# Other order of the first block's maxima, and one query tile summed among the first scores

## The chip, the core and the metric

The kernel runs on one core of one Trainium2 chip. The metric is the device time of one execution in microseconds (us), the median of several runs. Five engines work side by side: TensorE (PE, with its weight loads shown apart as PEld), VectorE (DVE), ScalarE (ACT), GpSimd (POOL) and SyncE (SP), which here issues the DMAs. Each engine works through its instructions in order and waits for the others through semaphores.

## The reference

Four attention layers follow one another, each added to its input: A, B, A, B. S = 2048 tokens, D = 576 features, H = 32 heads of Dh = 18.

```python
def _A_ref(x, wqkv, wo):                      # 32 key heads
    qkv = (x @ wqkv).reshape(B, S, 3, H, Dh).transpose(2, 0, 3, 1, 4)
    q, k, v = qkv[0], qkv[1], qkv[2]
    p = softmax(einsum("bhqd,bhkd->bhqk", q, k) * Dh ** -0.5)
    o = einsum("bhqk,bhkd->bhqd", p, v)
    return o.transpose(0, 2, 1, 3).reshape(B, S, D) @ wo
# _B_ref: the same with one key head and one value head for all 32 query heads
x = x + _A_ref(layernorm(x), A_wqkv, A_wo)
x = x + _B_ref(layernorm(x), B_wq, B_wk, B_wv, B_wo)
x = x + _A_ref(layernorm(x), A_wqkv, A_wo)
x = x + _B_ref(layernorm(x), B_wq, B_wk, B_wv, B_wo)
```

## The kernel before, in words

The program is written out by hand in the order in which each engine is to work; tiles come from pools with a fixed number of buffers, and a tile that finds no free buffer waits for the reader that frees one. Layers 0 and 2 are of kind A (`is_a`), layers 1 and 3 of kind B.

**A layer in three stages.** First the layer norm's scaled rows are transposed (`scaled`, `trans`; the rows' buffers have the tag `xh`, two of them) into `xts[T]`, four groups T of 512 tokens, and multiplied by the weights. `project(T, t)` (line 432) makes one tile of 128 features by 512 tokens. Each operand is held as a high and a low part, so a tile takes the 14 matmuls of `TERMS` (line 439). ACT copies the sum out (line 447, the high part), a second copy by ACT (line 453) and a subtraction on POOL (line 454) give the low part where the tile is a `filler`, and `store` (lines 499 to 503) writes both to the DRAM buffer `qk_d`: 512 KB for the high part, written twice, and 256 KB for the low one. `load_k`, `load_q` and `load_part` (line 545) bring heads from there into `big`.

Second, the attention loop goes over 16 pairs of heads (a = 0, 1) and four blocks u of 512 queries: 64 blocks w. A block needs the maximum of every score row first. `max_mm` (line 581) makes 128 queries by 512 keys on TensorE (line 613) and reduces them on DVE (line 620); from the third block on some pairs of key blocks are combined with the help of ACT (lines 605, 610, 617). A block has 32 maxima, 16 for each head; (qc, kb) is its part of the queries and its block of keys. After the 32nd, `max_final` makes the negated maxima (line 752), `max_store` transposes them (line 761) and stores them in four small DMAs to `m_d` (line 763), and `max_rows` loads them as rows of `big` (line 767). Then `exp_mm` computes scores with the maxima already subtracted (line 776), ACT takes the exponential (line 785), and `pv_block` sums the values into the PSUM bank `oacc` (line 806). Maxima run ahead of the exponentials by `LEAD` steps, and the value sums lag behind them by `LAG` = 1152 columns, so in the first slots of `UNIT` no value sum is there yet. A slot such as `em` says what each head does (e: a score and its exponential, m, d, t: a maximum), and the number behind it how many columns of value sums follow.

Third, `out_proj` multiplies by the output weights.

**The fill.** The last projections (`fill`) and the maxima that run ahead are woven: `woven(max_pairs, left, every)` lets a burst of four maxima go out after every so many matmuls of the fill. In a layer A it holds eight half value projections (63 units of one 512 column matmul) and four tiles of the last token group (`rest`, 56 units), with 14 bursts; in a layer B two tiles (28 units) and four bursts, and ten bursts lie in the projections before that. `FREE` is the number of units left behind the last burst.

**PSUM banks.** Score tiles come from two tags: `mtile` with three banks, `etile` with four. In a burst before the loop the fourth maximum takes an e bank, the other three m banks. Fill tiles and the scores of `exp_mm` take e banks.

**Order in a layer B.** `m_first` (line 576) gives the order of the maxima of the first two blocks. The keys of the fourth block are made by the first projection of T = 3 and loaded right behind it; bursts come twice in each of the next two projections. `max_store(0, 0)` goes out after 46 maxima and `max_rows(0, 0)` after 50.

**The tile `side`** has the tag `xx`, one buffer, which it shares with `xts[3]`; it holds some exponentials, the combined maxima and the copied value sums, and is taken after the fill.

Of the kernel before, what the change touches and what calls it, by code (L numbers as in the profile page):

```python
# [8 lines left out]
F32 = mybir.dt.float32  # L9
F32R = mybir.dt.float32r  # L10
AF = mybir.ActivationFunctionType
OP = mybir.AluOpType
# [6 lines left out]
P = 128  # L19
NCH = S // P  # L20
NPAIR = H // 2
# [9 lines left out]
TERMS = [(c, c) for c in range(4)] + [(c, 5 + c) for c in range(4)] + [(4, 4), (4, 9)] + [(5 + c, c) for c in range(4)]  # L31
# [13 lines left out]
STEPS = 8  # L45
LEAD = 14

FREE = 4
NM_AT = 3
ROW_AT = 5  # L50
SUM_AT = 4
# [18 lines left out]
LAG = 1152  # L70
# [57 lines left out]
def tile_kernel(ctx: ExitStack, tc: tile.TileContext, A_x, A_wqkv, A_wo, B_x, B_wq, B_wk, B_wv, B_wo, out):  # L128
    nc = tc.nc
# [4 lines left out]
    pool = ctx.enter_context(tc.tile_pool(name="pool", bufs=2))  # L134
# [26 lines left out]
    oacc = psum.tile([P, 512], F32, name="oacc")  # L161
# [27 lines left out]
    def etile(name):  # L189
        return psum.tile([P, 512], F32, tag="e", bufs=4, name=name)  # L190

    def ptile(name, shape=(P, 512), dt=F32):
        return pool.tile(list(shape), dt, tag="p", bufs=15, name=name)

    def xtile(name, shape=(P, 2, 9, 256), dt=F32R):
        return pool.tile(list(shape), dt, tag="xx", bufs=1, name=name)
# [61 lines left out]
    def wtile(t):  # L258
        return parts[(0, 2, 1)[t // 3]][:, t % 3]
# [36 lines left out]
    def woven(f, left, every):  # L296
        assert not weave["left"]
        weave.update(f=f, left=left, every=every, n=0)
# [55 lines left out]
    xts = {}  # L354
# [65 lines left out]
    for layer in range(4):  # L420
        is_a = layer % 2 == 0
# [72 lines left out]
        def store(ev_f, r0, r1, c0, t0):  # L494

            dst = qk_d[c0:c0 + r1 - r0, :, t0:t0 + 512]
            hi, lo = ev_f[0][r0:r1, None, :].to_broadcast([r1 - r0, 2, 512]), ev_f[1][r0:r1, :]
            if c0 < D:
                nc.sync.dma_start(dst[:, 0:3:2], hi)
                nc.sync.dma_start(dst[:, 1], lo)  # L500
            else:
                nc.sync.dma_start(dst[:, 0:2], hi)
                nc.sync.dma_start(dst[:, 2], lo)
# [65 lines left out]
        mxs, nms, pts, ocs = {}, {}, {}, {}  # L569

        def ops(p):
            return big[:, q_slot(p)], big[:, k_slot(p)]

        diffs, m_next, m_done, m_count = ([], []), [0, 0], [0], {}

        m_first = [] if is_a else ([(0, i // 2, i % 2) for i in range(8)] + [(1, i // 2, i % 2) for i in range(4)] +
                                   [(0, i, 2) for i in range(4)] + [(1, i // 2, i % 2) for i in range(4, 6)] +
                                   [(0, i, 3) for i in range(4)] + [(1, i // 2, i % 2) for i in range(6, 8)] +
                                   [(1, i, 2) for i in range(4)] + [(1, i, 3) for i in range(4)])

        def max_mm(a, tile):

            n = m_next[a]
            w, i = divmod(n, 16)
            shared = w >= FIRST_SHARED
            kind = "m"
            if n < len(m_first):
                w, qc, kb = m_first[n]
            elif shared:
                kind, qc, kb = MAX_OPS[a][i]  # L590
            else:
                qc, kb = PLAIN[i]
            p, u = divmod(w, 4)
            q, k = ops(p)
            if (p, u) not in mxs:
                mxs[p, u] = mxd[w % 2] if shared else pool.tile([P, 32], F32, name="mx")
            mx = mxs[p, u]
            b = 64 * a
            c0 = u * 512 + qc * P
            r0 = 16 * a + 4 * qc + kb  # L600
            m_next[a] += 1
            m_done[0] += 1
            if kind == "d":
                ps = etile("psd")
                nc.tensor.matmul(ps, q[b:b + 3 * DH, c0:c0 + P], kds[p if is_a else 0][b:b + 3 * DH],  # L605
                                 start=True, stop=True)
                r = side[:, n_r[0] % 4]
                n_r[0] += 1
                diffs[a].append(r)
                nc.scalar.activation(r, ps, AF.Relu)  # L610
            else:
                ps = tile("psm")
                nc.tensor.matmul(ps, q[b:b + KM, c0:c0 + P], k[b:b + KM, kb * 512:(kb + 1) * 512],  # L613
                                 start=True, stop=True)
                if kind == "t":
                    r = diffs[a].pop(0)
                    nc.vector.tensor_tensor_reduce(out=r, in0=ps, in1=r, scale=1.0, scalar=-3.0e38, op0=OP.add,  # L617
                                                   op1=OP.max, accum_out=mx[:, r0:r0 + 1])
                else:
                    nc.vector.reduce_max(mx[:, r0:r0 + 1], ps, axis=AX.X)  # L620
            m_count[p, u] = m_count.get((p, u), 0) + 1
            if m_count[p, u] == 32:
                max_final(p, u)

        def max_pair():
            if is_a and m_done[0] % 4 == 0:
                run_todo(m_done[0] // 4)
            for a in range(2):
                max_mm(a, etile if m_done[0] % 4 == 3 else mtile)
            if not is_a and m_done[0] == 46:  # L630
                max_store(0, 0)
            elif not is_a and m_done[0] == 50:
                max_rows(0, 0)


# [56 lines left out]
                for h, ps in enumerate(project_v(c)):  # L692
                    nc.scalar.activation(v_dst(c)[:, h], ps, AF.Copy)

        rest = [1, 2, 3, 5] if is_a else [2, 3]
        for T in range(4):
            if T == 0 and not is_a:
                fixed_rows(k_slot(0), True)
# [39 lines left out]
        fill = []  # L738
# [3 lines left out]
                    fill.append((project_v_part, (c, h)))  # L742
        for t in rest:
            fill.append((project, (3, t, True)))

        if is_a:
            load_k(0, 1536, S)
# [2 lines left out]
        def max_final(p, u):  # L750
            neg = pool.tile([P, 8], F32, name="neg")
            nc.vector.tensor_reduce(neg, mxs.pop((p, u)).rearrange("p (b k) -> p b k", k=4), axis=AX.X, op=OP.max,  # L752
                                    negate=True)
            hl = nms[p, u] = hls[(4 * p + u) % 2]
            copy(nc.gpsimd, hl[:, 0:8], neg)
            nc.gpsimd.tensor_tensor(hl[:, 8:16], neg, hl.bitcast(F32)[:, 0:8], op=OP.subtract)  # L756
# [13 lines left out]
        def exp_mm(p, u, i, tile):  # L770

            a, kc = (i // 2) % 2, i // 4 * 2 + i % 2
            q, k = ops(p)
            e = tile("pse")
            r = 64 * a
            nc.tensor.matmul(e, k[r:r + KE, kc * P:(kc + 1) * P], q[r:r + KE, u * 512:(u + 1) * 512],  # L776
                             start=True, stop=True)

            n_p[0] += 1
            r = n_p[0] // 5 % 3  # L780
            own = n_p[0] % 5 or (p, u) == (NPAIR - 1, 3) or sided.get(r) in pts
            pt = pts[p, u, i] = ptile("pt") if own else side[:, 6 + r]
            if not own:
                sided[r] = p, u, i
            nc.scalar.activation(pt, e, AF.Exp, scale=SCALE)  # L785
# [3 lines left out]
        def pv_cols(cols):  # L789

            while cols:
                n, c0 = divmod(pv_at[0], 512)
                w = min(cols, 512 - c0)
                pv_block(n, c0, c0 + w)
                pv_at[0] += w
                cols -= w
# [83 lines left out]
        def run_todo(st):  # L880
            for n in sorted(n for n in todo if n <= st):
                for f, args in todo.pop(n):
                    f(*args)
# [4 lines left out]
        at(b - 1, out_rows, 1)  # L888
        left = LEAD - m_done[0] // 4
        work = len(TERMS) * sum(288 / 512 if f is project_v_part else 1 for f, _ in fill)  # L890
        woven(max_pairs, left, (work - FREE) / left)
        for f, args in fill:
            f(*args)
        assert not weave["left"]
        side = xtile("side", (P, 9, 512), F32)
        late, n_e, n_r, n_p, sided = LAG, 0, [0], [0], {}
        for w in range(4 * NPAIR):
            p, u = divmod(w, 4)
            more_m = w < 4 * NPAIR - 2
            e_next = [0, 0]  # L900
            for kinds, cols in UNIT if more_m else ENDS if w == 4 * NPAIR - 2 else LAST:
                run_todo(LEAD + STEPS * w + sum(e_next) // 4)
                for a in range(2):
                    if kinds[a] == "e":
                        n = e_next[a]
                        e_next[a] += 1
                        exp_mm(p, u, n // 2 * 4 + 2 * a + n % 2, mtile if m_done[0] == 4 * ns and n_e % 7 % 2 else etile)
                        n_e += 1
                    else:
                        max_mm(a, mtile)  # L910
                skip = min(late, cols)
                late -= skip
                pv_cols(cols - skip)
            assert e_next == [16, 16]
        assert not diffs[0] and not diffs[1]
# [39 lines left out]
```

## Time and profile before

| | |
|---|---|
| median of 3 runs | 5605.41 us (5603.79 to 5609.56) |
| the profiled execution's own time | 5606.94 us |
| its span | 5605.2 us |
| mean granted TensorE clock | 0.999 |
| DVE busy | 4943.0 us, 88% |
| ACT busy | 4936.3 us, 88% |
| POOL busy | 1741.9 us, 31% |
| DMA | 291.59 MB, 52 GB/s over the span |

The profile shows one execution. Rows of its timeline read: start in us, duration in us, engine, line of the kernel, operation, output tile from input tiles, shapes, how many instructions were merged into the row; in brackets the idle time of the engine before them and what ended it. Times count from the start of the span. SPq rows are DMAs being issued; they land later. Windows give the busy time of each engine in a stretch, with the number of instructions. A DMA rate row gives GB/s in 40 equal slices of its window.

### The profile page before, as it was taken

Reading aid. Unit: us, or ns where it says so; the run is one execution under the profiler, and the core shown is the slowest. Engines: PE = TensorE matmul, PEld = TensorE weight load, DVE = VectorE, ACT = ScalarE, POOL = GpSimd, SP = SyncE. Lnnn points to the kernel's source line nnn. Section 1 sums busy time; section 2 is a strip of 40 time slices with the busy share of each in tenths; the row PEclk is TensorE's granted clock in tenths of the full one; section 3 lists DMA queues with packets and bytes.
Section 4 is the critical chain, followed back from the end, with each engine's and each line's share of the span. In section 5 each row is a group of like instructions: output and inputs, shape, how many; then the busy total and the mean of one; then the engine's idle time right before and its main releaser. Section 6 shows DMA issues by size and latency. Waiting matters only on the chain.

```text
span 5605.2 us, 138270 instructions
## 1 busy us (share of the span) xinstructions
PE 5579.4 (100%) x53372; PEld 2835.7 (51%) x53372; DVE 4943.0 (88%) x9513; ACT 4936.3 (88%) x9884; POOL 1741.9 (31%) x2236
## 2 busy tenths in 40 slices
PE   9999999999999999999999999999999999999999
PEld 7644444444844444444686444444448444444446
DVE  5799999998699999999747999999987999999995
ACT  3599999999389999999726999999992999999996
POOL 3142323234233232333421332323242333333332
PEclk9999999999999999999999999999999999999999
DMA  6311111111421000001253111111114201010102
GB/s 226 120 47 38 37 39 36 39 36 27 128 68 24 23 21 23 20 23 25 61 188 104 50 36 38 37 39 36 37 31 136 56 23 24 23 24 20 24 14 80
DMA packets 258556, 291.59 MB, mean 52 GB/s; under 512 B 132700, under 2 KB 172892, under 8 KB 248176
## 3 DMA queue, kind: packets, MB, share of 16 engines
q1 hardware_dynamic: 257896, 282.75, 18.0%
q8 instruction: 419, 6.86, 0.5%
q14 instruction: 241, 1.97, 0.1%
HBM read 158.77 MB, written 119.86 MB: 50 GB/s over the span
## 4 chain that ended last, share of the span: by engine, by line
PE 97%; ACT 1%; DVE 1%; DMA 0%; issue 0%; SPq 0%; POOL 0%; ACTq 0%; DVEq 0%; POOLq 0%
PE oacc L806 38%; PE pse L776 23%; PE psm L613 21%; PE psn L280 6%; PE psq L439 6%; PE psd L605 3%; ACT pt L785 1%; PE ps L272 0%; DVE mx L620 0%; DMA big<-m_d 0%; DMA m_d<-tr 0%; PE oacc L273 0%; SPq L763 0%; DVE mxd L620 0%; ACT side L785 0%
## 5 line engine op out<-in xcount | busy, mean ns | idle before, releaser
L620 DVE TENSOR_REDUCE mxd<-psm 128x1 f32<-128x512 f32 x5952 | 3750.1, 683 | 181.5 <-PE psd L605 64.9
L785 ACT ACTIVATE pt<-pse 128x512 f32<-128x512 f32 x6584 | 3578.4, 628 | 28.3 <-PE pse L776 1.5
L613 PE MATMUL psm<-big 62*128 62x512 f32 x7200 | 2504.4, 444 | 0.6
L776 PE MATMUL pse<-big 64*128 64x512 f32 x8192 | 2409.1, 431 | 7.2 <-DMA big<-m_d 3.1
L806 PE MATMUL oacc<-pt,vbuf 128*19 128x192 f32 (+6 forms) x20244 | 1794.5, 379 | 1.2 <-DVE oc L202 1.0
L776 PEld LDWEIGHTS pse<-big 64*128 64x128 f32 x8192 | 1209.2, 184 | 893.8 <-ACT pt L785 517.6
L613 PEld LDWEIGHTS psm<-big 62*128 62x128 f32 x7200 | 1132.7, 184 | 676.7 <-DVE mxd L620 262.2
L806 PE MATMUL oacc<-side,vbuf 128*19 128x64 f32 (+6 forms) x5004 | 1402.5, 377 | 0.0
L785 ACT ACTIVATE side<-pse 128x512 f32<-128x512 f32 x1608 | 998.4, 621 | 5.9
L202 POOL TENSOR_SCALAR hl<-neg 128x8 fp32r<-128x8 f32 x256 | 50.5, 197 | 2746.7 <-DVE neg L752 2746.7
L806 PEld LDWEIGHTS oacc<-pt,vbuf 128*19 128x19 f32 x20244 | 447.8, 97 | 604.8 <-issue 488.7
L617 DVE CUSTOM_DVE_ANT_0 side<-psm,side 128x512 f32<-128x512 f32 x992 | 681.1, 687 | 37.0 <-PE psm L613 8.6
L610 ACT ACTIVATE side<-psd 128x512 f32<-128x512 f32 x992 | 601.3, 648 | 1.3 <-PE psd L605 1.3
L806 PE MATMUL oacc<-pt,vy 128*19 128x384 f32 (+2 forms) x5700 | 587.2, 417 | 0.0
L829 POOL TENSOR_TENSOR rl<-lt,mone 128x8 f32<-128x8 f32 x256 | 422.9, 1652 | 350.2 <-DMA lt<-os 350.2
L806 PE MATMUL oacc<-side,vy 128*19 128x384 f32 (+2 forms) x1404 | 455.7, 415 | 0.0
L605 PE MATMUL psd<-kd,big 54*128 54x512 f32 x992 | 428.0, 472 | 0.0
L806 PEld LDWEIGHTS oacc<-side,vbuf 128*19 128x19 f32 x5004 | 317.4, 97 | 146.4 <-issue 119.8
L447 ACT ACTIVATE ev<-psq 128x512 fp32r<-128x512 f32 (+1 forms) x112 | 66.9, 598 | 319.1 <-PE psq L439 266.6
L842 POOL TENSOR_TENSOR os<-os,rb 96x512 f32<-96x512 f32 x256 | 328.2, 1282 | 19.8 <-DMA rb<-r_d 19.8
L820 POOL TENSOR_TENSOR os<-os,side 96x512 f32<-96x512 f32 x240 | 307.2, 1280 | 20.0
L202 POOL TENSOR_SCALAR os<-side 32x512 f32<-32x512 f32 x480 | 293.7, 612 | 40.1 <-POOL hl L756 0.4
(93 smaller groups left out, 3310.3 us busy)
## 6 DMA issues: line engine op xcount, KB each, us to landing
big<-qk_d SPq DMA_DIRECT2D x180, 432.0 KB
qk_d<-ev SPq DMA_DIRECT2D x96, 512.0 KB
qk_d<-ev SPq DMA_DIRECT2D x120, 256.0 KB
rb<-r_d SPq DMA_DIRECT2D x512, 36.0 KB
o_d<-os SPq DMA_DIRECT2D x512, 36.0 KB
m_d<-tr SPq DMA_DIRECT2D x1024, 2.0 KB
o<-o_d SPq DMA_DIRECT2D x64, 256.0 KB
big<-m_d SPq DMA_DIRECT2D x512, 4.0 KB
```

The costliest lines, as they stand in the source:

```text
L202: eng.tensor_scalar(dst, src, 1.0, 0.0, op0=OP.mult, op1=OP.add)
L280: nc.tensor.matmul(ps, lhs[:, xc, :], wsm[:, wc, h * 288:(h + 1) * 288], start=i == 0, stop=i == len(TERMS) - 1)
L439: nc.tensor.matmul(ps[:n].rearrange("p (u t) -> p u t", u=2)[:, us], w[:, wc, :n], xts[T][:, us, xc, :], start=(xc, wc) == TERMS[0], stop= ...
L605: nc.tensor.matmul(ps, q[b:b + 3 * DH, c0:c0 + P], kds[p if is_a else 0][b:b + 3 * DH], start=True, stop=True)
L610: nc.scalar.activation(r, ps, AF.Relu)
L613: nc.tensor.matmul(ps, q[b:b + KM, c0:c0 + P], k[b:b + KM, kb * 512:(kb + 1) * 512], start=True, stop=True)
L617: nc.vector.tensor_tensor_reduce(out=r, in0=ps, in1=r, scale=1.0, scalar=-3.0e38, op0=OP.add, op1=OP.max, accum_out=mx[:, r0:r0 + 1])
L620: nc.vector.reduce_max(mx[:, r0:r0 + 1], ps, axis=AX.X)
L776: nc.tensor.matmul(e, k[r:r + KE, kc * P:(kc + 1) * P], q[r:r + KE, u * 512:(u + 1) * 512], start=True, stop=True)
L785: nc.scalar.activation(pt, e, AF.Exp, scale=SCALE)
L806: nc.tensor.matmul(oacc[j:j + DH + 1, cs], v_of(kc)[:, 2 * p + a if is_a else 0, :], pts[p, u, i][:, cs], start=kc < 2 and c0 == 0, stop=k ...
L829: nc.gpsimd.tensor_tensor(rl, lts.pop((p, u)), mone, op=OP.pow)
```

## The change

In a layer A the tile t = 3 of the last token group is taken out of the fill (`held`), and the order of the others changes (5, 1, 2). Its 14 matmuls go out in two halves of seven in the loop's first two slots that have columns of value sums to skip: the first half behind the third score, the second behind the fifth. They sum in `oacc`; ACT copies the sum twice, into two buffers of the scaled rows' tag `xh`, POOL subtracts, and two DMAs store it. `side`, which shares its buffer with `xts[3]`, is taken only after that; until then an exponential takes a buffer of its own. `FREE` becomes 8 in a layer A, so the 14 bursts are spread over 97 of 105 units instead of 115 of 119.

In a layer B the maxima of the first two blocks go key block by key block, and the first block has its 32nd after 40 maxima instead of 44; its store and load go out after 42 and 48. The fourth key block is read from the 33rd maximum on instead of the 37th.

In both kinds the first maximum of a burst, not the fourth, takes the e bank.

```diff
-FREE = 4
+FREE = 8, 4
...
-        m_first = [] if is_a else ([(0, i // 2, i % 2) for i in range(8)] + [(1, i // 2, i % 2) for i in range(4)] +
-                                   [(0, i, 2) for i in range(4)] + [(1, i // 2, i % 2) for i in range(4, 6)] +
-                                   [(0, i, 3) for i in range(4)] + [(1, i // 2, i % 2) for i in range(6, 8)] +
-                                   [(1, i, 2) for i in range(4)] + [(1, i, 3) for i in range(4)])
+        def block(u, kb, qcs=range(4)):
+            return [(u, qc, kb) for qc in qcs]
+
+        m_first = [] if is_a else (block(0, 0) + block(0, 1) + block(1, 0) + block(0, 2) + block(0, 3) +
+                                   block(1, 1) + block(1, 2) + block(1, 3))
...
-                max_mm(a, etile if m_done[0] % 4 == 3 else mtile)
-            if not is_a and m_done[0] == 46:
+                max_mm(a, mtile if m_done[0] % 4 else etile)
+            if not is_a and m_done[0] == 42:
                 max_store(0, 0)
-            elif not is_a and m_done[0] == 50:
+            elif not is_a and m_done[0] == 48:
                 max_rows(0, 0)
...
-        rest = [1, 2, 3, 5] if is_a else [2, 3]
+        rest = [5, 1, 2, 3] if is_a else [2, 3]
...
         for t in rest:
             fill.append((project, (3, t, True)))
+        held = fill.pop()[1][1] if is_a else None
+
+        def held_part(i):
+            for n in range(7 * i, 7 * i + 7):
+                xc, wc = TERMS[n]
+                nc.tensor.matmul(oacc.rearrange("p (u t) -> p u t", u=2), wtile(held)[:, wc], xts[3][:, :, xc, :],
+                                 start=n == 0, stop=n == 13)
+            if i:
+                hi, lo = [pool.tile([P, 640], F32R, tag="xh", bufs=2, name="hev")[:, :512] for _ in range(2)]
+                nc.scalar.activation(hi, oacc, AF.Copy)
+                nc.scalar.activation(lo.bitcast(F32), oacc, AF.Copy)
+                nc.gpsimd.tensor_tensor(lo, lo.bitcast(F32), hi.bitcast(F32), op=OP.subtract)
+                store((hi.bitcast(F32), lo.bitcast(F32)), 0, P, held * P, 3 * 512)
...
-            own = n_p[0] % 5 or (p, u) == (NPAIR - 1, 3) or sided.get(r) in pts
+            own = n_p[0] % 5 or (p, u) == (NPAIR - 1, 3) or sided.get(r) in pts or side is None
...
-        woven(max_pairs, left, (work - FREE) / left)
+        woven(max_pairs, left, (work - FREE[layer % 2]) / left)
...
-        side = xtile("side", (P, 9, 512), F32)
+        side = None if is_a else xtile("side", (P, 9, 512), F32)
...
                 skip = min(late, cols)
                 late -= skip
+                if side is None and skip:
+                    held_part(int(late < LAG - 256))
+                    if late < LAG - 256:
+                        side = xtile("side", (P, 9, 512), F32)
                 pv_cols(cols - skip)
```

## The prediction

> **What bounds the kernel now.** I read the page's engine shares first, then the windows of one attention loop, then the first microseconds of the four loops in the timeline, because everything the change touches lies there.
>
> ```profile
> PE 5579.4 (100%) x53372; PEld 2835.7 (51%) x53372; DVE 4943.0 (88%) x9513; ACT 4936.3 (88%) x9884; POOL 1741.9 (31%) x2236
> 217.10:223.30 6.20, 5.40 (x28) 2.30 (x28) 5.94 (x10) 6.18 (x13) 1.29 (x1) 1.00 0.51 179
> 260.00:1000.00 740.00, 740.00 (x7620) 334.07 (x7618) 704.69 (x1349) 735.18 (x1468) 244.04 (x302) 1.00 0.16 40
> ```
>
> The second and third rows (columns: PE, weight load, DVE, ACT, POOL, clock, DMA share, GB/s) are the start and the middle of layer 0's loop. PE shows 100% in the middle, but it is a modelled busy time; ACT has 735.18 of 740 us. In the first 6.20 us PE has room (5.40), while ACT has none (6.18). So the gap on TensorE at the loop's start, where no value sums run yet, is a gap on TensorE alone: ACT is filled there by the exponentials.
>
> Does time lost by ACT at the start come back later? The loops do the same work, so I compare the lengths of three, from the first score matmul to the last long run of exponentials.
>
> ```profile
> 217.15 0.52 PE L776 MATMUL pse<-big 64*128 64x512 f32 x2
> 1390.68 15.53 ACT L785 ACTIVATE pt<-pse 128x512 f32<-128x512 f32 x31
> 1558.91 0.73 PE L776 MATMUL pse<-big 64*128 64x512 f32 x4 [0.65 <-DMA big<-m_d]
> 2735.20 15.53 ACT L785 ACTIVATE pt<-pse 128x512 f32<-128x512 f32 x31
> 3028.92 0.70 PE L776 MATMUL pse<-big 64*128 64x512 f32 x3 [0.64 <-DMA big<-m_d]
> 4352.15 0.90 PE L776 MATMUL pse<-big 64*128 64x512 f32 x4 [0.47 <-DMA big<-m_d]
> 5524.84 16.51 ACT L785 ACTIVATE pt<-pse 128x512 f32<-128x512 f32 x33
> 1565.00:1570.00 5.00, 5.00 (x34) 1.70 (x26) 2.10 (x4) 2.25 (x5) 0.09 (x1) 0.50 0.58 151
> ```
>
> Layer 0: 1173.5 us, layer 1: 1176.3, layer 3: 1172.7. Layer 1 ran some microseconds at clock 0.50 (last row; ACT busy only 2.25 of 5.00) and is 3.6 us longer than layer 3. A loss in the first 15 us was still there 1,100 us later. I therefore charge every microsecond that ACT loses at a loop's start to the total, one for one.
>
> **Layers 0 and 2, the fill.** Before the loop, projections are woven with bursts of four maxima.
>
> ```profile
> 177.08 2.00 PE psn L280 x15
> 213.09 2.13 PE L439 MATMUL psq<-xx,big 128*128 128x512 f32 x8
> 215.15 0.73 PE L613 MATMUL psm<-big 62*128 62x512 f32 x4
> 215.69 3.08 DVE L620 TENSOR_REDUCE mx<-psm 128x1 f32<-128x512 f32 x5 [0.24 <-PE psm L613]
> 212.96 2.48 DVE L620 TENSOR_REDUCE mx<-psm 128x1 f32<-128x512 f32 x4 [0.24 <-PE psm L613]
> 215.82 1.20 PE L439 MATMUL psq<-xx,big 128*128 128x512 f32 x4
> 216.95 0.49 PE L613 MATMUL psm<-big 62*128 62x512 f32 x1
> 80.84 3.28 PE psq L439 x14
> ```
>
> The fill lasts from 177.08 to 216.95, 39.9 us. Fourteen projection matmuls (3.28 us, last row) leave it. With work 105 and FREE 8 a burst comes every 6.93 units instead of 8.21. Eight units take 215.15 - 213.09 = 2.06 us, so 6.93 take 1.80; with the burst's 0.67 (215.15 to 215.82) the period on TensorE falls from 2.7 to 2.47 us. DVE needs 2.48 us a burst, so the two are now even, and then the banks decide. Three maxima of a burst go to the three m banks, one to an e bank. Before, the fourth took the e bank, so a burst waited at most for reduction three of the burst before; after, maxima two to four take the m banks, and the fourth waits for reduction four. That the bank rule holds is seen in layer 3, where DVE lags:
>
> ```profile
> 4346.47 11.05 DVE L620 TENSOR_REDUCE mx<-psm 128x1 f32<-128x512 f32 x18
> 4346.57 1.10 PE L613 MATMUL psm<-big 62*128 62x512 f32 x4
> ```
>
> The burst at 4346.57 takes 1.10 instead of 0.73: its third maximum waits for the reduction that ends at about 4347.1. In the new order reduction four ends 0.53 + 2.48 us after a burst's start, the next burst's fourth matmul can start 0.07 later, and 0.35 + 1.80 later comes the following burst: two periods make 5.23, one 2.62. Fill after: 13 small matmuls 1.75, 13 periods 34.1, a last burst with its wait 0.97, eight free matmuls 2.06: 38.9 us, a gain of 1.0 us. If the banks cost nothing: 1.75 + 13 x 2.47 + 0.67 + 2.06 = 36.6, a gain of 3.3. I take 1.0, since the wait follows from the rows.
>
> **Layers 0 and 2, the held tile.** Let T be the first maximum after the fill (216.95 before).
>
> ```profile
> 217.12 0.60 ACT L447 ACTIVATE ev<-psq 128x512 fp32r<-128x512 f32 x1 [3.90 <-PE psq L439]
> 217.61 0.59 ACT L453 ACTIVATE evr<-psq 128x512 f32<-128x512 f32 x1
> 218.09 2.08 ACT L785 ACTIVATE pt<-pse 128x512 f32<-128x512 f32 x4
> 219.78 1.09 PE L613 MATMUL psm<-big 62*128 62x512 f32 x2
> 222.60 0.95 PE L806 MATMUL oacc<-pt,vbuf 128*19 128x448 f32 x8
> ```
>
> Before, ACT starts two copies at T+0.2 and T+0.7, exponentials from T+1.1 at 0.49 us each; the sixth starts near T+3.5. After: three scores go out by T+0.7; seven held matmuls (1.6 us, with the switch 1.8) fill TensorE until T+2.5; scores four and five follow, and reach ACT 0.59 later (1558.91 to 1559.50 in layer 1 and 4352.15 to 4352.74 in layer 3), at T+3.1 and T+3.6, where ACT had been free since T+2.6. Seven more matmuls end at T+5.0. The next two instructions of ACT are the copies of the held sum (hi, lo), so it waits until T+5.1, copies until T+6.1, and starts its sixth exponential there: 2.5 us later than before. Of this 1.0 is the copies, which in the fill lay in ACT's idle time (3.90 us before `ev`), and 1.5 is waiting behind the held matmuls. DVE and the value sums (222.60) shift with it. The subtraction goes to POOL, which idles there. SP's lo store waits for it; behind it stand the key difference of pair 1 and the second block's tiny stores, which SP issued only at 227.85, T+10.9, so the wait (to about T+7.5) is covered. Costing nothing by the same measure: key tile 5 going first in the fill, one more exponential in its own buffer, and the sum in `oacc` and the scaled rows' buffers, whose last readers ended before the fill. Sum: 2.5 - 1.0 = **+1.5 us a layer**; without the bank wait -0.8.
>
> **Layers 0 and 2, the held tile's stores.** They write 512 + 256 KB and now stand ahead of the 2 KB stores of the second block's maxima.
>
> ```profile
> 227.85 1.69 SPq L763 DMA_DIRECT2D m_d<-tr  x4
> 234.29 0.52 SPq L767 DMA_DIRECT2D big<-m_d  x2
> 236.06 0.70 PE L776 MATMUL pse<-big 64*128 64x512 f32 x3
> 3019.98 1.69 SPq L763 DMA_DIRECT2D m_d<-tr  x4
> 3027.15 0.52 SPq L767 DMA_DIRECT2D big<-m_d  x2
> ```
>
> The load at 234.29 had to wait for the tiny store, which took 4.7 us to land (5.5 in layer 2): the queue is backed up. The next block's scores followed at 236.06 with nothing to spare, and in layer 2 they waited 0.64 (3028.92 above). 0.77 MB more take between 2.1 us (at 373 GB/s, the best slice at that start) and 4.3 us (at the 179 of the first window); the scores are due 2.5 us later themselves. Bounds over both layers: from -0.6 (layer 2's wait goes) to +4.2; I take +1.5.
>
> ```profile
> GB/s 105 0 0 136 373 220 319 161 175 134 166 45 192 158 150 99 147 159 189 168 145 182 231 136 158 90 11 25 77 23 63 39 102 56 169 192 147 192 181 136
> ```
>
> **Layers 1 and 3, the order of the maxima.** The first block ends four maxima earlier, so its store and row load leave a burst earlier; the 0.65 and 0.47 us waits for big<-m_d go. But the fourth key block is now needed at the 33rd maximum instead of the 37th.
>
> ```profile
> 4334.42 1.22 SPq L545 DMA_DIRECT2D big<-qk_d  x2
> 4337.02 0.73 PE L613 MATMUL psm<-big 62*128 62x512 f32 x4
> 4337.55 7.47 DVE L620 TENSOR_REDUCE mx<-psm 128x1 f32<-128x512 f32 x12 [0.51 <-PE psm L613]
> 4339.28 0.73 PE L613 MATMUL psm<-big 62*128 62x512 f32 x4
> GB/s 301 134 217 217 251 117 201 234 167 167 234 251 184 167 217 168 184 251 184 184 167 267 268 284 217 267 217 167 217 234 234 251 184 268 217 435 418 401 401 401
> ```
>
> The two loads of that block are issued from 4334.42 on. The burst at 4339.28 is the first that reads it and does not wait, so it has landed by then; the new order reads it at 4337.02. The last row is the DMA rate from 4334.4 to 4339.3 in 40 slices: near 220 while loads and stores mix, over 400 once only stores are left, from slice 36 on, at 4338.7. So I put the landing at 4338.7 to 4339.1 and the stall of TensorE, which works in order, at 2.0 us (bounds 0 and 2.26). DVE, which from 4337.55 on never waits again until the first scores, loses about 1.8 of it; the rest of the fill follows DVE through the banks. Walking the six bursts with the rule above, the first score moves from 4352.15 to 4353.8, past the row load that now lands before it, and the first exponential from 4352.74 to about 4354.5: **+1.8 us a layer**, between -0.5 (keys in time, only the wait gone) and +2.2.
>
> **Sum.** 2 x 1.5 + 1.5 + 2 x 1.8 = +8.1 us. The profiled execution took 5606.94 (span 5605.2, 1.7 around it), with one half-clock stretch in it; the median of three runs is 5605.41. On the profiled execution the sum gives 5615.0, on the median **5613.5**. All lower bounds together give -3.2 (5602), all upper ones +11.6 (5617).
>
> **Rivals.** (1) *The gap is free.* If the loop is bound by TensorE and not by ACT, 3.28 us leave each of two fills, return into idle time, and ACT catches up. PE's 100% speaks for it, layer 1's 3.6 us that ACT never regained against it. Time: -2 x 3.28 for layers 0 and 2, stores hidden, + 2 x 1.8 for 1 and 3 = -3.0, that is 5602.4, not slower. (2) *The clock drops in the stall.* Layer 1 went to 0.50 after a stretch in which TensorE was never idle longer than 0.65 us but thinly loaded; the new 2 us stall in layers 1 and 3 leaves a like stretch of 3.4 us only 40% loaded. Each drop costs what layer 1 paid, 3.6: 8.1 + 3.6 to 8.1 + 7.2, 5617 to 5621; it decides as soon as one drop is added. The held matmuls make a drop in layers 0 and 2 less likely, but neither shows one now. The Trainium skill (TensorE: Matmul & The Clock Gate, Why this matters for your kernels) asks for no idle gap over about 3 us between bursts, by which a 2 us stall would be harmless and the sum would stay at +8.1. Layer 1 dropped with a far shorter gap, so by this trace the page's limit is too wide. (3) *The keys land in time*, because the loads go out earlier than now: layers 1 and 3 gain 0.5 each, total +3.5, 5609. Against it: nothing ahead of the load changes.
>
> **How the numbers follow.** Forecast 0.60, rival (1) 0.10, rival (2) 0.20, rival (3) 0.10. A measurement tells about 0.2%, 11.2 us, from no change. The forecast, (1) and (3) lie within it except for the forecast's upper edge; (2) lies beyond. Faster by over 0.2%: 0.02; slower by over 0.2%: 0.22; within: 0.76. The range runs from 5603 (most of rival 1 left out) to 5621.
>
> **What would show it.** In layers 0 and 2 the fill ends about 1 us sooner, bursts come about 2.6 us apart, and ACT stands idle twice before `hi`, 0.5 and 1.0 us; the second block's first scores wait for big<-m_d. In layers 1 and 3 a burst of maxima waits about 2 us for big<-qk_d, and the first scores wait for no DMA. The loop lengths of layers 0 and 2 grow by 2.5 us and more. Wrong would be: bursts 2.47 apart, no wait for big<-qk_d, or loops of layers 0 and 2 as long as now.

## The result and the profile after

The changed kernel took a median of 5614.32 us (21 runs, 5610.72 to 5619.19) and the kernel before 5605.12 us (21 runs on the same chip, 5603.79 to 5610.19): 9.2 us more, a ratio of 1.0014 with a 95% interval of 1.0009 to 1.002. The profiled execution of the changed kernel has a span of 5617.2 us.

The engine shares of the page after, and two rows of PE's waits in its trace (us in total, times, longest):

```profile
PE 5588.9 (99%) x53372; PEld 2841.9 (51%) x53372; DVE 4945.9 (88%) x9513; ACT 4937.3 (88%) x9884; POOL 1742.8 (31%) x2236
...
PE pse L790 <- DMA big<-m_d: 5.4, 6, 1.4
PE psm L614 <- DMA big<-qk_d: 1.5, 4, 0.5
```

Every engine has as many instructions as before (53372, 9513, 9884, 2236), and DVE, ACT and POOL are busy only 1 to 3 us longer, so no work was added: the 9 us are waiting. PE's busy time grew by 9.5 us (5579.4 before), in part because a burst whose matmuls wait for a bank shows as one longer row, as below. The last row is new. It is the fourth key block in layers 1 and 3, the predicted one, but 1.5 us in both layers together where 2.0 in each were forecast.

**Layers 0 and 2.** The timeline of the changed kernel, layer 0, from the last bursts of the fill to the first long run of exponentials:

```profile
210.48 0.88 PE L614 MATMUL psm<-big 62*128 62x512 f32 x4
211.01 2.48 DVE L621 TENSOR_REDUCE mx<-psm 128x1 f32<-128x512 f32 x4 [0.21 <-PE psm L614]
213.12 0.93 PE L614 MATMUL psm<-big 62*128 62x512 f32 x4
...
215.81 0.72 PE L790 MATMUL pse<-big 64*128 64x512 f32 x3
216.46 1.89 PE L751 MATMUL oacc<-xx,big 128*128 128x512 f32 x7
216.94 1.58 ACT L799 ACTIVATE pt<-pse 128x512 f32<-128x512 f32 x3
218.81 1.09 ACT L799 ACTIVATE pt<-pse 128x512 f32<-128x512 f32 x2 [0.28 <-PE psm L614]
218.93 1.89 PE L751 MATMUL oacc<-xx,big 128*128 128x512 f32 x7
220.86 0.60 ACT L755 ACTIVATE hev<-oacc 128x512 fp32r<-128x512 f32 x1 [0.97 <-PE oacc L751]
221.36 0.59 ACT L756 ACTIVATE hev<-oacc 128x512 f32<-128x512 f32 x1
221.83 2.08 ACT L799 ACTIVATE pt<-pse 128x512 f32<-128x512 f32 x4
```

The bursts start 2.64 us apart, and each takes 0.88 or 0.93 instead of 0.73: its last maximum waits for a bank. Below, ACT makes five exponentials, waits 0.28 and 0.97 us behind the two halves of the held tile, copies the sum, and begins the sixth exponential only at 221.83.

**Layers 1 and 3.** The same view of layer 3, from the burst ahead of the key block to the first exponentials:

```profile
4338.42 1.31 PE L614 MATMUL psm<-big 62*128 62x512 f32 x4
4339.09 1.22 SPq L545 DMA_DIRECT2D big<-qk_d  x2
4342.59 0.46 PE L614 MATMUL psm<-big 62*128 62x512 f32 x1 [0.25 <-DMA big<-qk_d]
4343.09 0.69 DVE L621 TENSOR_REDUCE mx<-psm 128x1 f32<-128x512 f32 x1 [1.38 <-PE psm L614]
4343.52 0.70 PE L614 MATMUL psm<-big 62*128 62x512 f32 x3 [0.47 <-DMA big<-qk_d]
4356.01 1.19 PE L614 MATMUL psm<-big 62*128 62x512 f32 x4
4358.27 0.73 PE L790 MATMUL pse<-big 64*128 64x512 f32 x3
4358.37 0.60 ACT L447 ACTIVATE ev<-psq 128x512 fp32r<-128x512 f32 x1 [4.49 <-PE psq L439]
4358.87 0.59 ACT L453 ACTIVATE evr<-psq 128x512 f32<-128x512 f32 x1
4359.34 2.08 ACT L799 ACTIVATE pt<-pse 128x512 f32<-128x512 f32 x4
```

The third and fifth rows wait for the two key loads, DVE stands idle 1.38 us before the first of its reductions, and the first scores (4358.27) wait for no DMA. Their exponentials begin only at 4359.34, since ACT first copies the last projection twice. The first row is the surprise: the burst *before* the stalled one already takes 1.31 us. The last burst before the scores (4356.01) is as stretched, 1.19.

To place the time I cut each layer's loop by start times of instructions in the timeline: stretch 1 from the first maximum of the run-ahead to the first exponential, stretch 2 from there to the sixth exponential, stretch 3 from the sixth to the 33rd, with which the second block begins. For instance, stretch 1 of layer 0 after runs from 178.55 to 216.94, and stretch 2 to 221.83:

```profile
178.55 0.73 PE L614 MATMUL psm<-big 62*128 62x512 f32 x4
```

An asterisk marks a stretch in which the granted clock was 0.50 for 3.41 or 6.83 us.

| kernel | layer 0 | layer 1 | layer 2 | layer 3 |
|---|---|---|---|---|
| before | 39.08 / 2.38 / 16.09 | 45.03 / 2.40 / 19.46* | 39.08 / 2.38 / 16.81 | 44.85 / 2.40 / 15.98 |
| after | 38.39 / 4.89 / 17.00 | 47.45 / 2.38 / 16.91 | 38.40 / 4.89 / 16.87 | 47.32 / 2.38 / 18.41* |
| e1 old banks | 36.05 / 5.96 / 15.91 | 47.45* / 2.39 / 17.72* | 36.05 / 5.96 / 15.91 | 46.00 / 2.39 / 15.99 |
| e2 order only | 39.09 / 2.39 / 16.61 | 45.90 / 2.39 / 16.87* | 39.08 / 2.39 / 17.20 | 46.05 / 2.39 / 15.99 |
| e3 old order | 38.37 / 4.93 / 17.21 | 46.75 / 2.40 / 15.99 | 38.34 / 4.93 / 15.91 | 46.70 / 2.40 / 16.39 |
| e4 early keys | 38.39 / 4.90 / 15.94 | 46.75 / 2.39 / 15.99 | 38.36 / 4.91 / 15.93 | 46.69 / 2.39 / 16.23 |
| e5 order, early keys | 39.06 / 2.38 / 16.40 | 44.29 / 2.38 / 16.00 | 39.08 / 2.38 / 17.52* | 44.41 / 2.38 / 16.01 |
| e6 copies on DVE | 36.04 / 5.49 / 18.22* | 44.41 / 2.38 / 16.00 | 36.05 / 5.49 / 16.97 | 44.33 / 2.38 / 16.78 |
| e7 held tile spread | 36.05 / 4.04 / 22.04* | 44.44 / 2.39 / 16.24 | 36.05 / 4.04 / 23.31* | 44.41 / 2.39 / 16.13 |
| e8 banks only | 39.60 / 2.38 / 18.67* | 46.89 / 2.40 / 16.20 | 39.69 / 2.38 / 18.52* | 46.67 / 2.38 / 16.00 |
| e9 late store | 38.39 / 4.89 / 15.95 | 47.43 / 2.38 / 16.37 | 38.37 / 4.93 / 16.15 | 47.38 / 2.38 / 16.13 |

From the 33rd exponential on, the loops are alike in all kernels (18.6 to 18.8 us to the 65th, and 1150.3 to 1151.9 from there to the last, but 1152.4 to 1153.7 where a half-clock interval falls near the end), and between the layers lie 108.5 us and 220.4 to 220.7 us in all. So the first two stretches hold what the change does. Stretch 3 scatters between 15.9 and 17.2 us without a drop of the clock, between executions of alike code too, and is read with care.

By this table a layer 0 or 2 costs 2.51 - 0.69 = 1.82 us more, a layer 1 2.42 and a layer 3 2.47. Twice 1.82 and 2.45 make 8.5 of the measured 9.2. The rest is less than the interval leaves open (0.0009 to 0.002 of 5605 is 5 to 11 us).

### The profile page after: what moved, and what is told of

Its sections match the earlier page's. It is cut to its first block, busy times and chain, and to the rows that moved or that the text cites. A ratio compares the mean times of both kernels' runs of the same rounds, so it can differ in the third digit from the quotient of the medians.

```text
span 5617.2 us, 138252 instructions
## 1 busy us (share of the span) xinstructions
PE 5588.9 (99%) x53372; PEld 2841.9 (51%) x53372; DVE 4945.9 (88%) x9513; ACT 4937.3 (88%) x9884; POOL 1742.8 (31%) x2236
## 4 chain that ended last, share of the span: by engine, by line
PE 95%; DVE 1%; DMA 1%; ACT 1%; SPq 0%; issue 0%; POOL 0%; POOLq 0%; ACTq 0%; DVEq 0%
PE oacc L820 38%; PE pse L790 22%; PE psm L614 21%; PE psn L280 6%; PE psq L439 5%; PE psd L606 3%; ACT pt L799 0%; DMA big<-qk_d 0%; DVE mx L621 0%; PE ps L272 0%; DMA big<-m_d 0%; DMA m_d<-tr 0%; DVE mxd L621 0%; PE oacc L751 0%; DMA qk_d<-ev 0%
## 5 line engine op out<-in xcount | busy, mean ns | idle before, releaser
L820 PE MATMUL oacc<-side,vbuf 128*19 128x64 f32 (+5 forms) x4996 | 1400.9, 377 | 0.2 <-ACT side L200 0.2
```

The lines of the kernel that those rows point to most:

```text
L820: nc.tensor.matmul(oacc[j:j + DH + 1, cs], v_of(kc)[:, 2 * p + a if is_a else 0, :], pts[p, u, i][:, cs], start=kc < 2 and c0 == 0, stop=k ...
```

## The experiments

The theory after the result: two producers of the fill are held back. The new bank order (the burst's *first* maximum in the e bank) lets TensorE run less far ahead of DVE; the fourth key block comes late; and the held tile keeps ACT idle. The rivals were that the gap on TensorE is worth nothing by itself, that the held tile's stores delay the second block, and that the clock is to blame. The nine kernels ran beside the kernel before on the same chips, 10 or 11 runs each; the medians of before there were 5605.6 (e1 to e4), 5606.16 (e5 to e7) and 5606.18 (e8, e9). The intervals of e1, e2 and e5 to e8 include 1, and that of e4 begins there, so what follows rests on the stretches, of one profiled execution each.

### e1: the changed kernel with the old bank order

```diff
-                max_mm(a, mtile if m_done[0] % 4 else etile)
+                max_mm(a, etile if m_done[0] % 4 == 3 else mtile)
```

> The changed kernel with the bank order of before (the fourth maximum of a burst takes the e bank again, not the first). Theory 1 (banks pace the fill): bursts in the fills of layers 0 and 2 come 2.47 us apart instead of 2.65, the first maximum after the fill comes 2 us sooner in each, and layers 1 and 3 gain some 0.4 us each: total about +4 us over the kernel before (5609). Theory 2 (VectorE paces the fill, the banks do not matter): bursts stay 2.6 us or more apart and the total stays at +9 us (5614).

5605.73 us, ratio 1.0 (0.9992 to 1.0009): with this one line back, the runs no longer tell the changed kernel from the kernel before. Both theories had forecast more (5609 and 5614). The timeline of its layer 0:

```profile
206.21 0.73 PE L614 MATMUL psm<-big 62*128 62x512 f32 x4
208.70 0.73 PE L614 MATMUL psm<-big 62*128 62x512 f32 x4
...
212.50 0.49 PE L790 MATMUL pse<-big 64*128 64x512 f32 x1 [0.57 <-ACT evr L453]
212.92 1.88 PE L751 MATMUL oacc<-xx,big 128*128 128x512 f32 x7
215.26 1.09 ACT L799 ACTIVATE pt<-pse 128x512 f32<-128x512 f32 x2 [1.34 <-PE psm L614]
```

Bursts take 0.73 again and come 2.49 apart, and the fill is 2.34 us shorter (36.05 for 38.39). But the e bank of the third score is now held by the last projection's copy (`evr`, 0.57 us), the held tile starts later, ACT waits 1.34, and the sixth exponential comes 5.96 instead of 4.89 after the first. Net gain 1.27 a layer. Not all of the cost is gone: stretches 1 and 2 together are still 0.55 us longer than before in layers 0 and 2, 1.14 in layer 3, and 2.41 in layer 1, where the clock dropped. The total hides this, probably in part by the clock: 5 of the 11 runs list a mean granted clock of 1.000, of the 33 of before beside them only 3.

### e2: the kernel before with the new order of the maxima alone

```diff
-        m_first = ... (the interleaved list; 46 and 50)
+        m_first = ... (key block by key block; 42 and 48)
```

> The kernel before with one part of the change: the new order of the first two blocks' maxima in layers 1 and 3 (store after 42, row load after 48). Bank order and layers 0 and 2 as before. Theory 1 (the fourth key block is read before it has landed): a burst waits about 2 us for big<-qk_d in each, the first exponential comes 1.4 us later: total +2.7 us (5607.8), range +1.5 to +3.8. Theory 2 (the loss in layers 1 and 3 comes from the banks, the order only removes the wait for big<-m_d): -1 us (5604).

5607.49 us, ratio 1.0005 (0.9996 to 1.0014). Stretch 1 of layers 1 and 3 is 45.90 and 46.05, that is 0.9 and 1.2 longer. The key loads and the burst that needs them, layer 3:

```profile
4331.11 1.22 SPq L545 DMA_DIRECT2D big<-qk_d  x2
4334.91 0.46 PE L614 MATMUL psm<-big 62*128 62x512 f32 x1 [1.12 <-DMA big<-qk_d]
4335.65 0.70 PE L614 MATMUL psm<-big 62*128 62x512 f32 x3 [0.27 <-DMA big<-qk_d]
```

TensorE waits 1.39 us here, not the 2 of the forecast. The 0.9 and 1.2 are less than half of what layers 1 and 3 lost in the changed kernel; e3 shows what else costs there.

### e3: the changed kernel with the old order of the maxima

```diff
-        m_first = ... (key block by key block; 42 and 48)
+        m_first = ... (the interleaved list; 46 and 50)
```

> The changed kernel with the old order of the maxima in layers 1 and 3 (46 and 50 again); held tile, FREE 8 and new bank order stay. Theory 1: layers 1 and 3 lose no more than about 0.5 us each through the banks; the total is that of layers 0 and 2, +4.5 to +6.5 us (5610 to 5612). Theory 2 (layers 1 and 3 carry the whole loss): within 1.5 us of before.

5610.52 us, ratio 1.0009 (1.0001 to 1.0018). The total came as expected, for a wrong reason: layers 1 and 3 should have lost at most 0.5 us and lost 1.72 and 1.85 (46.75 and 46.70) with no late key block at all. So the bank order alone costs there what I had put on the keys.

### e4: the changed kernel with the key block's loads issued ahead of the query store

```diff
                 store(ev_f, 96, 96 + DH, D, t0)
+                if T == 3:
+                    load_k(0, t0, t0 + 512)
                 store(ev_f, 0, 64, 512, t0)
...
-                if not is_a and i < 2:
+                if not is_a and i < 2 and (T, i) != (3, 0):
```

> The changed kernel, in layers 1 and 3 with the load of the fourth key block issued ahead of the 384 KB store of the queries that stood before it in SP's queue. Theory 1 (the 2 us wait is the landing of that load): the wait for big<-qk_d falls from 2 us to under 0.7 us and the first exponential comes 1 to 1.8 us sooner in each: total +5.5 to +7 us (5611 to 5612). Theory 2 (TensorE waits there for something else): wait and total unchanged, +9 us (5614).

5610.97 us, ratio 1.0009 (1.0 to 1.0018). PE's waits for big<-qk_d are gone, yet stretch 1 shrinks only by 0.70 and 0.63 where 1 to 1.8 were expected, to the 46.75 and 46.70 of e3. Its timeline, layer 3:

```profile
4332.01 1.31 PE L616 MATMUL psm<-big 62*128 62x512 f32 x4
4335.85 0.73 PE L616 MATMUL psm<-big 62*128 62x512 f32 x4
4338.11 1.31 PE L616 MATMUL psm<-big 62*128 62x512 f32 x4
```

The 1.31 us bursts have no key wait in them. They come where six projections stand between two bursts: DVE needs 2.48 us for a burst's four reductions, and the last maximum waits for the fourth reduction of the burst before.

### e5: the new order of the maxima and the early keys, with the old banks and no held tile

```diff
 (the kernel before)
-        m_first = ... (the interleaved list; 46 and 50)
+        m_first = ... (key block by key block; 42 and 48)
+                if T == 3:
+                    load_k(0, t0, t0 + 512)
...
-                if not is_a and i < 2:
+                if not is_a and i < 2 and (T, i) != (3, 0):
```

> The kernel before with the new order of the maxima in layers 1 and 3 and the key load ahead of the queries' store there; bank order and layers 0 and 2 as before. Theory 1 (of the order's loss nothing is left once the keys land in time): no wait for big<-qk_d nor for the first big<-m_d, and the first exponential comes 44.3 to 44.6 us after the first maximum instead of 44.85 to 45.03: total -1 us (5604.5). Theory 2 (the order costs something by itself): 45.5 us or more, total +1 to +2 us.

5601.66 us, ratio 0.9992 (0.9983 to 1.0001), the lowest median of all. Stretch 1 of layers 1 and 3 is 44.29 and 44.41, 0.74 and 0.44 shorter than before. The timeline, layer 3:

```profile
4338.31 13.41 DVE L623 TENSOR_REDUCE mx<-psm 128x1 f32<-128x512 f32 x22
4345.42 0.73 PE L779 MATMUL pse<-big 64*128 64x512 f32 x2
4346.49 2.08 ACT L788 ACTIVATE pt<-pse 128x512 f32<-128x512 f32 x4
```

DVE reduces 22 maxima without a gap, and the first scores wait neither for keys nor for the row of maxima. So the new order by itself is a gain once its keys are in time. The version is faster than the changed kernel (the intervals to before don't touch: up to 1.0001 here, from 1.0009 there); against the kernel before the interval still holds 1. Of the 4.5 us between the medians the stretches show only 1.2 (0.74 + 0.44). The rest probably goes with the clock: 8 of the 11 runs list a mean granted clock of 1.000, of the 27 of before beside them 1; among the runs at 0.999 the medians are 5605.05 (3 runs) and 5605.99 (22).

### e6: old banks, early keys, and the held sum's copies on DVE

```diff
 (the changed kernel with the edits of e1 and e4)
-                nc.scalar.activation(hi, oacc, AF.Copy)
-                nc.scalar.activation(lo.bitcast(F32), oacc, AF.Copy)
-                nc.gpsimd.tensor_tensor(lo, lo.bitcast(F32), hi.bitcast(F32), op=OP.subtract)
+                copy(nc.vector, hi, oacc)
+                nc.vector.tensor_tensor(lo, oacc, hi.bitcast(F32), op=OP.subtract)
```

> Held tile in two halves, FREE 8, new order of maxima, old bank order, key load ahead of the queries' store; and the held sum is copied and subtracted by VectorE instead of copied twice by ACT and subtracted by POOL. Theory 1 (ACT's loss at the loops' start in layers 0 and 2 is 1.0 us of copies and the rest waiting behind the held matmuls): the sixth exponential comes 5.0 us after the first instead of 5.96 with ACT's copies; layers 0 and 2 end up about 0.5 us shorter each than in the kernel before, total -2 us (5603.5). Theory 2 (the copies lie in ACT's idle time): 5.9 us as before them, total 0.

5603.02 us, ratio 0.9994 (0.9985 to 1.0003). The sixth exponential came 0.47 us sooner than in e1 (5.49 after the first), not 0.96. The timeline, layer 0:

```profile
217.77 0.69 DVE L202 TENSOR_SCALAR hev<-oacc 128x512 fp32r<-128x512 f32 x1 [0.74 <-PE oacc L753]
218.25 2.06 ACT L800 ACTIVATE pt<-pse 128x512 f32<-128x512 f32 x4 [1.46 <-PE psm L616]
219.84 1.19 PE L616 MATMUL psm<-big 62*128 62x512 f32 x2 [0.99 <-DVE mx L623]
```

ACT no longer copies, but still waits 1.46 us behind the held matmuls, and now DVE is late with its reductions: TensorE waits 0.99 for `mx`. The cost of the copies moved to the next engine. The total was near the 5603.5 of the forecast by another way: layers 0 and 2 were to end up 0.5 us shorter than before and are 0.07 longer by stretches 1 and 2 (41.53 for 41.46), and layers 1 and 3 are 0.6 and 0.5 shorter, as in e5.

### e7: old banks, early keys, and the held tile in nine small pieces

```diff
 (the changed kernel with the edits of e1 and e4)
+HELD = 0, 4, 1, 1, 1, 1, 2, 1, 1, 2
...
-                if side is None and skip:
-                    held_part(int(late < LAG - 256))
+                if side is None:
+                    held_part(HELD[s])
```

> Held tile, FREE 8, new order of maxima, old bank order, key load ahead of the queries' store; the 14 held matmuls go out in nine pieces (4 1 1 1 1 2 1 1 2 behind the slots 2 to 10) instead of two sevens, and ACT's copies follow the twelfth score. Theory 1 (two thirds of ACT's loss is waiting behind blocks of seven): from the first to the sixth exponential 2.4 to 3.0 us instead of 5.96, the copies and the later value sums cost 1.0 to 2.2 us after that; layers 0 and 2 are 0.8 to 1.5 us shorter each than in the kernel before, total -2.5 to -4 us (5601.5 to 5603). Theory 2 (TensorE's work in that stretch is what counts, however it is cut): from the first to the 33rd exponential 21.9 us as with two sevens.

5609.05 us, ratio 1.0004 (0.9995 to 1.0013); the theory that small pieces would fit into idle time (5601.5 to 5603) fell, and so did its rival: from the first to the 33rd exponential it takes 26.08 and 27.35 us, not 21.9. The sixth exponential does come sooner (4.04), but stretch 3 grows to 22.04 and 23.31. The timeline of layer 0, a row of PE's waits, and the window of the half clock (busy time of PE, weight load, DVE, ACT and POOL, then clock, DMA share, GB/s):

```profile
221.64 0.60 ACT L761 ACTIVATE hev<-oacc 128x512 fp32r<-128x512 f32 x1
222.12 0.62 ACT L762 ACTIVATE hev<-oacc 128x512 f32<-128x512 f32 x1
225.04 1.09 ACT L614 ACTIVATE side<-psd 128x512 f32<-128x512 f32 x2 [2.31 <-PE psd L609]
...
PE oacc L826 <- ACT hev L762: 3.1, 2, 1.6
223.07:226.48 3.41, 3.41 (x26) 1.20 (x22) 1.47 (x3) 1.44 (x3) 1.01 (x1) 0.50 0.82 283
```

The value sums need `oacc` themselves and wait for the copies (3.1 us in two layers), ACT idles 2.31, and TensorE ran at half clock for 3.41 us from 223.07 on, within that idle time; in layer 2 it did so for 6.83 us. How the loss divides between the waits and the clock is open. By the prices of a drop given at the end (1.45 us for 3.41 and 3.5 for 6.83) some 4 us a layer above the 16 of most other rows would be left for the waits, an estimate. None of the placements tried here (two halves, DVE's copies, nine pieces) left the loop's start without a delay.

### e8: the kernel before with the new bank order alone

```diff
-                max_mm(a, etile if m_done[0] % 4 == 3 else mtile)
+                max_mm(a, mtile if m_done[0] % 4 else etile)
```

> The kernel before with one part of the change: the first maximum of a burst takes the e bank, not the fourth. Theory 1 (the bank order alone carries most of the loss in layers 1 and 3, where VectorE lags): the first exponential there comes 46.6 to 46.8 us after the first maximum instead of 44.9 to 45.0; in layers 0 and 2, whose bursts come 2.7 us apart, it stays at 39.1 within 0.2: total +3.5 us (5609.5). Theory 2 (the banks cost only together with the late keys): 45.5 us or less, total +1 us.

5611.18 us, ratio 1.0008 (0.9999 to 1.0017). Stretch 1 grows by 0.52 and 0.61 in layers 0 and 2, where at most 0.2 was expected, and by 1.86 and 1.82 in layers 1 and 3, as expected. Layer 3 of the kernel before first, then of e8:

```profile
4333.75 0.74 PE L613 MATMUL psm<-big 62*128 62x512 f32 x4
```

```profile
4337.84 1.30 PE L613 MATMUL psm<-big 62*128 62x512 f32 x4
4342.22 4.88 DVE L620 TENSOR_REDUCE mx<-psm 128x1 f32<-128x512 f32 x8 [1.09 <-PE psm L613]
4343.95 1.29 PE L613 MATMUL psm<-big 62*128 62x512 f32 x4
4347.76 2.48 DVE L620 TENSOR_REDUCE mx<-psm 128x1 f32<-128x512 f32 x4 [0.67 <-PE psm L613]
```

Where before a burst took 0.74, it takes 1.30, and DVE, which reduced from 4337.55 on without a wait before, now stands idle 1.09 and 0.67 us. The two gaps make 1.76 us, nearly the whole loss of layer 3. With e3 and e4, whose layers 1 and 3 lose nearly the same, this shows the share of the banks.

### e9: the changed kernel with the held tile's stores put off

```diff
-                store((hi.bitcast(F32), lo.bitcast(F32)), 0, P, held * P, 3 * 512)
+                at(LEAD + 8, store, (hi.bitcast(F32), lo.bitcast(F32)), 0, P, held * P, 3 * 512)
```

> The changed kernel with the 768 KB store of the held tile put off to the step in which the second block's exponentials begin, behind the maxima's small stores and row loads. Theory 1 (the held store delays the second block's maxima): from the sixth to the 33rd exponential 15.9 us in layers 0 and 2 instead of 17.0 and 16.9, total 2 us less than the changed kernel (5612). Theory 2 (the queue is backed up by the key and query loads anyway; the stretch varies from run to run): between 15.9 and 17.2 as in all runs, total 5614.

5613.76 us, ratio 1.0013 (1.0004 to 1.0023): as slow as the changed kernel. In the timeline of layer 0 the held store now follows the row load and the scores that read it:

```profile
230.08 0.52 SPq L781 DMA_DIRECT2D big<-m_d  x2
234.58 0.69 PE L790 MATMUL pse<-big 64*128 64x512 f32 x3
235.48 0.39 SPq L499 DMA_DIRECT2D qk_d<-hev  x1
```

The changed kernel issues that load at 234.75 and starts these scores at 238.33, after a wait of 0.86, and ACT stands idle 0.94 behind it. Stretch 3 is 15.95 and 16.15 here for 17.00 and 16.87, as the first theory said, but the total didn't fall by its 2 us, and e4, whose layers 0 and 2 are the changed kernel's with the same early stores, has 15.94 and 15.93 and no such wait. The kernel before has 16.09 and 16.81, and the same two layers in e2 16.61 and 17.20. So the stores delay the load, but whether the scores then wait differs between executions of the same code, and no loss against the kernel before is seen.

## Why the prediction was right, and where it was not

The forecast of 5613.5 met 5614.32, inside the range, with the sign of the sum right. Step by step:

- **ACT's loss is charged in full: right.** The sixth exponential came 2.51 us later after the first (4.89 for 2.38), forecast 2.5, by the forecast route: two waits and two copies. The waits were 0.28 and 0.97 for 0.5 and 1.0. Nothing of it came back in the 1,150 us behind it, so rival (1), the free gap, fell.
- **The fill: rule right, gain too high by 0.3.** Bursts 2.64 apart were forecast as 2.62. The fill gained 0.69 us for 1.0. Without the bank wait it would have gained 3.03 (e1, 36.05 for 39.08), forecast 3.3. A layer 0 or 2 thus came to +1.82, forecast +1.5.
- **The held tile's stores: wrong, +1.5 forecast, none seen.** The step took a later row load for a later block. The load did get later and its scores did wait 0.86 us, but e4, with the same early stores, and e9, with late ones, have the same stretch 3 within 0.2 us. A loss smaller than the scatter of that stretch stays open.
- **Layers 1 and 3: size too low, cause half seen.** +1.8 was forecast and +2.45 measured. The prediction started from the late keys, with a DVE that loses 1.8 of the stall and banks that pass this on. But banks alone cost 1.7 to 1.9 (e3, e8), and the new order alone 0.9 to 1.2 (e2). The two losses overlap: late keys cost 1.6 with the old banks (e2 less e5) and 0.6 to 0.7 with the new (the changed kernel less e4). With its keys in time the order gives 0.4 to 0.7 back with the old banks (e5) and nothing with the new (e4 for e8). Two steps fell short. The walk over six bursts had the first score 1.65 us later; in layer 3 it came 1.99 later (46.25 us after the first maximum for 44.26). It began at the stalled burst, as if the bursts ahead were as in the trace of before. In fact the bank rule, which I had applied to layers 0 and 2, already stretched the burst before it (1.31 at 4338.42). And from the first score to the first exponential I had put 0.7, near the 0.59 of before, where that score had waited for big<-m_d while ACT copied the last projection. Without that wait the copies end last, and the step takes 1.07 (4358.27 to 4359.34).
- **The stall: 2.0 forecast, about 1.2 measured.** Behind the six projections that began at 4340.67 (row below) the burst would have run from 4342.3 for 0.73 us; it ended at 4344.2, some 1.2 later, of which the two wait records show 0.25 + 0.47. The burst before had been 0.58 longer already (1.31 for 0.73), and this hid part of the loads' time.

```profile
4340.67 1.67 PE L439 MATMUL psq<-xx,big 128*128 128x512 f32 x6
```

- **The sum: right partly by errors that cancel.** Per kernel, -1.5 (stores), +0.6 (fill and held tile) and +1.3 (layers 1 and 3) make +0.4: 8.1 forecast, 8.5 by the table. A forecast of the total this near says less than it seems.
- **Rival (3), keys in time, fell** by the wait row. **Rival (2), the clock, is real and didn't decide.** In the changed kernel's own trace no drop follows the stall. It did strike in the predicted place in e1, layer 1, after 4 us in which TensorE was busy 2.61; the waits of the stalled burst were 0.79 and 0.59 us. The rows: the stalled burst, then the windows ahead of the drop and in it.

```profile
1542.62 0.46 PE L614 MATMUL psm<-big 62*128 62x512 f32 x1 [0.79 <-DMA big<-qk_d]
1543.68 0.78 PE L614 MATMUL psm<-big 62*128 62x512 f32 x3 [0.59 <-DMA big<-qk_d]
...
1540.00:1544.00 4.00, 2.61 (x14) 1.67 (x12) 2.45 (x5) 1.06 (x2) 1.27 (x1) 1.00 0.86 255
1544.15:1547.56 3.41, 3.41 (x10) 2.13 (x10) 1.89 (x3) 0.00 (x0) 0.00 (x0) 0.50 0.28 100
```

Stretch 1 is 47.45 there and 46.00 in layer 3 of the same run: 1.45 us for 3.41 us at half clock; the 3.6 that I had priced were for a drop of 6.83. The Trainium skill (TensorE: Matmul & The Clock Gate, Why this matters for your kernels) asks to avoid idle gaps over about 3 us; this drop came behind shorter ones, so here too that limit is too wide. The mean granted clock of every run tells that the clock doesn't carry the result. Of the changed kernel's 21 runs 9 list 1.000 (median 5612.43) and 12 list 0.999 (5615.01); of the 79 runs of before beside the experiments 5 list 1.000 (5603.03), 68 list 0.999 (5605.99) and 6 list 0.998. At like clock the difference is about 9 us in both rows, and the changed kernel loses less clock than before, not more.

## What to carry to other kernels

Which item of a burst takes the spare bank sets how far the producer may run ahead of a consumer that is nearly as busy: here moving it from the last item to the first cost 1.8 us in each of two layers, and in the fill it took back 2.3 of 3.0 us gained. A gap on the busiest engine is free space only if the engine behind it is idle there too; ask that engine's row before filling it. Walk a queue of bursts from the first one under the new rule, not from the first one that waits, and read freshly stored data back ahead of stores that nobody waits for.

## What the runs showed of the hardware

I had not expected the half clock so often. It showed in the stretches of eight of the eleven kernels of the table (the asterisks), always 0.50 and for 3.41 or 6.83 us. In e8 it came at 219.75 and 3015.26, places at which the kernel before, with the same loop there, ran at full clock. Its price was 1.45 us for 3.41 in e1's layer 1 and 3.5 for 6.83 in layer 1 of before (19.46 against 15.98). What decides where it falls stays open. The time from the start to the first maximum also differs between executions: 176.1 to 177.0 us in nine profiles, and 178.55 and 179.01 in the two (after and before) that have a half-clock interval at 51 us. Differences of a few us between single profiles of this kernel are therefore read stretch by stretch, not from the span.
